# Top-k attention and a tanh-shrink layer on one core: weights turned by VectorE in 32x32 blocks, value products on eight tiles of TensorE

## The chip, the cores and the metric

The program runs on one core of one Trainium2 chip. The metric is device time in microseconds (us) for one execution, from the first to the last instruction with what the launch adds around it. A change under 0.2% of this kernel's time can't be told from no change.

A core has four engines that compute, TensorE (matrix products and transposes), VectorE, ScalarE and GpSimd, and a fifth, SyncE, that here only issues DMAs. Each works through its own instructions in order and waits on semaphores for the others. The profile calls them PE, DVE, ACT, POOL and SP; PEld is TensorE's loading of the stationary operand, which it lists apart from the products.

## The reference

Two blocks, one after the other, all in float32. The first is attention over 8 batches, 8 heads, 576 positions and head size 64, which keeps for each query the 32 largest scores; the second is a feed-forward layer of width 2048 on the 4608 rows of 512.

```python
scores = scale * np.matmul(q, k.transpose(0, 1, 3, 2))
kth = np.partition(scores, -top_k, axis=-1)[..., -top_k:-top_k + 1]
scores = np.where(scores >= kth, scores, -1000000000.0)
attn = np.exp(scores - np.max(scores, axis=-1, keepdims=True))
attn = attn / (np.sum(attn, axis=-1, keepdims=True) + 1e-09)
attn_out = np.matmul(attn, v)
x = attn_out.transpose(0, 2, 1, 3).reshape(4608, 512)
h = x @ w_in
out = (h - np.tanh(h)) @ w_out
```

## The kernel before

**Steps.** The unit of attention is a step: 128 queries of one pair of heads `hp` in one batch `b`. A batch has four pairs. 576 queries are four blocks of 128 (`qt` 0 to 3) and a rest of 64; a rest step (`rem`) takes the 64 last queries of two head pairs together. That makes 18 steps for a batch (16 and two rests) and 144 in all. `plan` (L462) puts them in order: for each batch the blocks 0 and 1 of the four pairs, then the two rest steps, then the blocks 2 and 3.

**A step's way through the engines.** `scores` (L198) forms 128 x 576 scores for both heads in four matmuls into the PSUM tile `scps`, and ScalarE copies them to `sc` (L215). `search` (L218) is VectorE's part: it splits the 576 keys into two halves, takes the larger and the smaller of each pair (L237, L238, which read `scps` and `sc`), and finds the threshold with four rounds of eight maxima (L245) and replacements (L248). `mask` (L255) sets what lies below the threshold far down (ScalarE L277, GpSimd L280), `expo` (L289) takes the exponential in place in `z` and its sum. `weigh` (L328) turns the 128 x 576 weights of each head so that keys lie on partitions: nine transposes on TensorE through PSUM (L346, L352), copied out by ScalarE to `et` and `e4` (L349, L353). `values` (L357) runs once for two blocks (256 queries) or for a rest step: for each head four matmuls with 128 keys and one with 64 (L374), the two heads side by side in the two column halves of the array, then one or two transposes that spread the reciprocal of the sums (L382), a copy (L386) and a product on GpSimd (L396).

**The feed-forward layer** works on units of 256 rows: 18 units, each 16 items `ffn_h` (four matmuls, L416) and 16 items `ffn_o` (two matmuls, L436). A unit becomes ready when the last pair of heads of its two blocks is through `values`. `deal` (L534) spreads its items over the steps that follow.

**Order.** The program's order is written out by hand in `run` (L485); there is no scheduler. In iteration `n` of its main loop each engine gets, in this order: the turning of step n-2 (first part), `mask` of n-1, `search` of n, four tenths of the step's feed-forward items, `scores` of n+1, the rest of the turning of n-2, `expo` of n-1, two tenths, `values` of n-2, two tenths, what is due in `todo` (loads, and the turning of keys and queries in `turn_kq`, L173), two tenths. `between(i)` is called in `search` after round i.

**The first 17 steps** also convert the feed-forward weights, which come as raw words: 32 pieces in all, one piece in each of the steps 0 to 8, four in step 9, three in each of the steps 10 to 16. A piece is two loads issued by ScalarE's queue (`raw` L117, `shifted` L119), and in a first part (part 1) VectorE L129 and L133 and ScalarE L130, L131, L136, in a second (part 2) VectorE L139 and GpSimd L142. Loads run three pieces ahead: when a piece's second part is through, the load of the third next is issued. Feed-forward items wait for the pieces that they need.

**Loads.** SyncE loads keys, queries and values for each pair of heads once (`load_kq` L156, eight DMAs; `load_v` L165, four DMAs). The values of a pair stay for all its steps, in four buffers.

Matmuls in float32 stand twice in the profile: L436 has 18 x 32 = 576 matmuls in the program and 1152 rows, each a load of the stationary operand and a product. Such a row is called a pass here. Transposes take one pass.

At the end VectorE checks that the search in halves found the true threshold everywhere; if not, everything is run again exactly. That second run does not take place with these inputs.

Of the kernel before, what the change touches and what calls it, by code (L numbers as in the profile page):

```python
# [19 lines left out]
J = 4  # L20
# [22 lines left out]
def kernel(  # L43
# [19 lines left out]
    CF = DFF // P  # L63
    WJ = 4
# [15 lines left out]
    mpool = pool("m", 3)  # L80
    zpool = pool("z", 2)
    etpool = pool("et", 1)
# [4 lines left out]
    rawpool = pool("raw", 3)  # L87
    shpool = pool("shifted", 3)
# [58 lines left out]

    raw, kT, qT, vb, vr = {}, {}, {}, {}, {}
# [4 lines left out]
    def main_rows(src, b, h):  # L153
        return src[b, h, 0:JP, :].rearrange("(p j) d -> p j d", j=J)

    def load_kq(b, hp):  # L156
        for name, src in (("k", k), ("q", q)):
            x = ldpool.tile([P, J + 1, 2, D], FP32, tag=f"{name}in", name=f"{name}in")
            for t in range(2):
                h = 2 * hp + t  # L160
                nc.sync.dma_start(x[:, 0:J, t, :], main_rows(src, b, h))
                nc.sync.dma_start(x[0:R, J, t, :], src[b, h, JP:S, :])
            raw[name, b, hp] = x

    def load_v(b, hp):  # L165
        x = vb[b, hp] = kqpool.tile([P, 2, J, D], FP32, tag="vb", name="vb")
        y = vr[b, hp] = kqpool.tile([P, D], FP32, tag="vr", name="vr")
        for t in range(2):
            h = 2 * hp + t
            nc.sync.dma_start(x[:, t, :, :], main_rows(v, b, h))  # L170
            nc.sync.dma_start(y[half(t), :], v[b, h, JP:S, :])

    def turn_kq(b, hp):  # L173
        p4 = None
        for name, dst in (("k", kT), ("q", qT)):
# [3 lines left out]
            for c in range(J):  # L179
# [3 lines left out]
            p4 = zt_ps.tile([P, 512], FP32, tag="zt", name="kqps")  # L183
            nc.tensor.transpose(  # L184
                p4[:, 0:R], x[0:R, J, :, :].rearrange("p h d -> p (h d)"), ident[0:R, 0:R]
            )

            for rows, o in [(half(0), 0), (half(1), R)] if name == "k" else [(slice(0, P), 0)]:
                nc.scalar.copy(d[rows, o : o + JP], ps[rows, :])
                o = 0 if o else JP  # L190
                nc.scalar.copy(d[rows, o : o + R], p4[rows, 0:R])
            yield

    st = {}

    def scores(n):  # L198
        g = steps[n]
        ps = sc_ps.tile([P, 2, 2, 512], FP32, tag="sc", name="scps")  # L200
        for s in range(2):
            ks = slice(s * S2, (s + 1) * S2)
            for i in range(2 if g.rem else 1):
                qs = slice(JP, S) if g.rem else slice(g.qt * P, (g.qt + 1) * P)
                rows = half(i) if g.rem else slice(0, P)
                for t in range(2):
                    nc.tensor.matmul(  # L207
                        ps[rows, t, s, 0:S2],
# [6 lines left out]
        nc.scalar.copy(sc[:], ps[:, :, :, 0:S2])  # L215
        st[n] = dict(sc=sc, ps=ps)

    def search(n, exact, between):  # L218
# [6 lines left out]
        sc, ps = x["sc"], x.pop("ps")  # L225
# [6 lines left out]
        else:  # L232
# [4 lines left out]
            nc.vector.tensor_tensor(lo, ps[:, :, 0, 0:S2], sc[:, :, 1, :], ALU.min)  # L237
            nc.vector.tensor_tensor(hi, ps[:, :, 0, 0:S2], sc[:, :, 1, :], ALU.max)  # L238
# [87 lines left out]
    ets = {}  # L326

    def weigh(n):  # L328


        g, z = steps[n], st[n]["z"]
        if g.rem:
            o = 0
        else:
            o = (g.qt % 2) * P
        if o:
            et, e4 = ets[n - 1]
        else:
            et = etpool.tile([P, 2, J, N], FP32, tag="et", name="et")
            e4 = etpool.tile([P, N], FP32, tag="e4", name="e4")  # L340
        ets[n] = et, e4
        for t in range(2):
            zt = zt_ps.tile([P, 512], FP32, tag="zt", name="zt")
            m0 = t * (S + R)
            for c in range(J):
                nc.tensor.transpose(  # L346
                    zt[:, c * P : (c + 1) * P], z[:, m0 + c * P : m0 + (c + 1) * P], ident[:]
                )
            nc.scalar.copy(et[:, t, :, o : o + P], zt[:].rearrange("p (c j) -> p c j", c=J))  # L349
# [135 lines left out]
    def run(exact):  # L485
# [32 lines left out]
        for piece in pieces[:3]:  # L518
            next(piece)
# [105 lines left out]
```

## Time and profile before

| | us |
|---|---|
| median of 3 runs (1764.85 to 1766.08) | 1765.44 |
| the profiled execution | 1765.89 |
| its span, first to last instruction | 1764.0 |

| engine | busy us | share of the span | instructions |
|---|---|---|---|
| PE | 1628.9 | 92% | 8418 |
| PEld | 1041.7 | 59% | 8418 |
| DVE | 1159.9 | 66% | 3635 |
| ACT | 1086.1 | 62% | 2133 |
| POOL | 893.2 | 51% | 1369 |

The groups that the change touches, of the list of the costliest groups (out<-in, count, busy us, mean ns of one):

| line, engine | what | count | busy us | mean ns |
|---|---|---|---|---|
| L346 PE | transposes of the weights | 1152 | 159.1 | 283 |
| L352 PE | the same, last 64 keys | 144 | 48.0 | 333 |
| L349 ACT | their copy out of PSUM | 288 | 156.8 | 597 |
| L353 ACT | the same, last 64 keys | 144 | 38.8 | 270 |
| L374 PE | value products, 128 keys | 1536 | 148.0 | 336 |
| L374 PE | value products, last 64 keys | 384 | 53.7 | 358 |
| L382 PE | spreading the reciprocals | 144 | 34.3 | 312 |
| L386 ACT | copy of products and reciprocals | 80 | 43.5 | 544 |

How to read it: an engine's busy time is the union of its instructions' spans, so where passes overlap, the mean of one is longer than what each adds. For TensorE the chain of waits is the better measure: it follows the end of the program back to what held each step up, and gives each pass the time by which it moved the chain on.

### The profile page before, as it was taken

Reading aid. Unit: us, or ns where it says so; the run is one execution under the profiler, and the core shown is the slowest. Engines: PE = TensorE matmul, PEld = TensorE weight load, DVE = VectorE, ACT = ScalarE, POOL = GpSimd, SP = SyncE. Lnnn points to the kernel's source line nnn. Section 1 sums busy time; section 2 is a strip of 40 time slices with the busy share of each in tenths; the row PEclk is TensorE's granted clock in tenths of the full one; section 3 lists DMA queues with packets and bytes.
Section 4 is the critical chain, followed back from the end, with each engine's and each line's share of the span. In section 5 each row is a group of like instructions: output and inputs, shape, how many; then the busy total and the mean of one; then the engine's idle time right before and its main releaser. Section 6 shows DMA issues by size and latency. Waiting matters only on the chain.

```text
span 1764.0 us, 25564 instructions
## 1 busy us (share of the span) xinstructions
PE 1628.9 (92%) x8418; PEld 1041.7 (59%) x8418; DVE 1159.9 (66%) x3635; ACT 1086.1 (62%) x2133; POOL 893.2 (51%) x1369
## 2 busy tenths in 40 slices
PE   3645669999999999999999999999999999999998
PEld 2324435657574757575666565757475756575664
DVE  5886777678767777733767786678766876752700
ACT  3766666657675767644666576757675767643631
POOL 1555654646454645542545464647454655542621
PEclk9777789999999999999999999999999999999999
DMA  5434422100210011000020002100110011000000
GB/s 179 129 108 174 171 102 58 30 13 1 50 44 13 1 46 48 8 7 13 21 53 21 13 8 53 34 13 1 47 47 7 7 34 47 6 7 13 1 12 14
DMA packets 106765, 73.03 MB, mean 41 GB/s; under 512 B 85632, under 2 KB 93824, under 8 KB 106624
## 3 DMA queue, kind: packets, MB, share of 16 engines
q1 hardware_dynamic: 97408, 37.78, 8.3%
q10 hardware_dynamic: 9216, 33.54, 5.3%
q8 instruction: 68, 1.11, 0.2%
q14 instruction: 73, 0.60, 0.1%
HBM read 61.85 MB, written 9.44 MB: 40 GB/s over the span
## 4 chain that ended last, share of the span: by engine, by line
PE 86%; DVE 7%; ACT 4%; issue 1%; ACTq 1%; POOL 0%; DMA 0%; SPq 0%; DVEq 0%; POOLq 0%
PE ops L436 28%; PE hps L416 27%; PE av L374 10%; PE scps L207 8%; PE zt L346 7%; DVE m L245 2%; PE zt L352 2%; PE av L382 2%; DVE ab L248 2%; DVE f L139 1%; PE kqps L180 1%; ACT sc L215 1%; ACT z L277 1%; PE kqps L184 1%; ACTq L119 0%
## 5 line engine op out<-in xcount | busy, mean ns | idle before, releaser
L280 POOL TENSOR_TENSOR z<-sc,z 128x576 f32<-128x576 f32 x288 | 401.8, 1417 | 283.0 <-ACT z L277 283.0
L436 PE MATMUL ops<-w_out,g 128*128 128x512 f32 x1152 | 530.3, 598 | 0.0
L416 PE MATMUL hps<-xT,w_in 128*128 128x256 f32 x2048 | 477.9, 384 | 0.0
L245 DVE MAX8 m<-ab 128x8 f32<-128x288 f32 (+1 forms) x1152 | 467.9, 448 | 0.0
L416 PEld LDWEIGHTS hps<-xT,w_in 128*128 128x128 f32 x2048 | 384.2, 194 | 47.6 <-issue 0.5
L248 DVE MATCH_REPLACE8 ab<-m,ab 128x288 f32<-128x288 f32 x864 | 375.8, 443 | 0.0
L436 PEld LDWEIGHTS ops<-w_out,g 128*128 128x128 f32 x1152 | 208.8, 194 | 192.0 <-issue 188.8
L430 POOL TENSOR_TENSOR g<-g,th 128x512 f32<-128x512 f32 x144 | 183.6, 1275 | 205.2 <-ACT g L429 200.5
L277 ACT ACTIVATE z<-sc,tbs 128x576 f32<-128x576 f32 x288 | 208.2, 775 | 51.7 <-POOL tbs L264 51.7
L293 ACT ACTIVATE z<-z,nb 128x576 f32<-128x576 f32 x288 | 222.7, 779 | 15.1 <-POOL z L280 15.1
L215 ACT COPY sc<-scps 128x1152 f32<-128x1152 f32 x144 | 160.3, 1113 | 116.3 <-ACT z L277 46.5
L349 ACT COPY et<-zt 128x512 f32<-128x512 f32 x288 | 156.8, 597 | 97.7 <-PE zt L346 97.3
L314 DVE RECIPROCAL rd<-rd 128x4 f32<-128x4 f32 x64 | 11.3, 177 | 310.2 <-POOL rd L307 310.1
L346 PE MATMUL zt<-ident,z 128*128 128x128 f32 x1152 | 159.1, 283 | 49.7 <-ACT z L293 29.8
L207 PE MATMUL scps<-kT,qT 64*128 64x288 f32 (+1 forms) x1280 | 188.1, 447 | 8.4 <-DVE ab L238 8.0
L237 DVE TENSOR_TENSOR ab<-scps,sc 128x576 f32<-128x576 f32 x144 | 106.6, 740 | 134.3 <-ACT sc L215 100.8
L346 PEld LDWEIGHTS zt<-ident,z 128*128 128x128 f32 x1152 | 139.9, 146 | 91.5 <-ACT z L293 31.6
L428 ACT ACTIVATE th<-hps 128x512 f32<-128x512 f32 x144 | 85.3, 593 | 144.5 <-PE hps L416 125.9
L207 PEld LDWEIGHTS scps<-kT,qT 64*128 64x128 f32 (+1 forms) x1280 | 101.0, 184 | 100.5 <-issue 33.9
L374 PE MATMUL av<-et,vb 128*64 128x256 f32 (+1 forms) x1536 | 148.0, 336 | 0.0
L374 PEld LDWEIGHTS av<-et,vb 128*64 128x64 f32 x1536 | 86.4, 139 | 62.3 <-ACT e L353 12.9
L240 DVE MAX8 ab<-ab 128x8 f32<-128x288 f32 x288 | 116.8, 447 | 0.0
(62 smaller groups left out, 1360.2 us busy)
## 6 DMA issues: line engine op xcount, KB each, us to landing
raw<-in_moe_w_in_dram ACTq DMA_DIRECT2D x16, 512.0 KB, 3.7
kin<-in_k_dram SPq DMA_DIRECT2D x64, 128.0 KB, 2.6
qin<-in_q_dram SPq DMA_DIRECT2D x64, 128.0 KB, 2.6
vb<-in_v_dram SPq DMA_DIRECT2D x64, 128.0 KB, 2.3
raw<-in_moe_w_out_dram ACTq DMA_DIRECT2D x16, 512.0 KB, 3.6
out_dram<-ot SPq DMA_DIRECT2D x32, 256.0 KB, 2.2
shifted<-in_moe_w_in_dram ACTq DMA_DIRECT2D x16, 511.5 KB, 4.6
shifted<-in_moe_w_out_dram ACTq DMA_DIRECT2D x16, 511.5 KB, 4.5
```

What stands on the lines that cost most here:

```text
L207: nc.tensor.matmul(ps[rows, t, s, 0:S2], qT[g.b, g.hp + i][half(t), qs], kT[g.b, g.hp + i][half(t), ks], start=True, stop=True,)
L215: nc.scalar.copy(sc[:], ps[:, :, :, 0:S2])
L245: nc.vector.max(m[:, t, m8], last[t] if i == rounds - 1 else cur[t])
L248: nc.vector.match_replace(nxt[t], m[:, t, m8], cur[t], NEG)
L277: nc.scalar.activation(zv[:, t, :], scf[:, t, :], AF.Relu, bias=tbs[:, t, n : n + 1], scale=-BIG)
L280: nc.gpsimd.tensor_tensor(zv[:, t, :], scf[:, t, :], zv[:, t, :], ALU.subtract)
L293: nc.scalar.activation(x["zv"][:, t, :], x["zv"][:, t, :], AF.Exp, bias=x["nb"][:, t : t + 1], scale=scale, accum_out=den[:, t : t + 1],)
L346: nc.tensor.transpose(zt[:, c * P : (c + 1) * P], z[:, m0 + c * P : m0 + (c + 1) * P], ident[:])
L374: nc.tensor.matmul(av[half(t), 0, cols], vb[g.b, hp][:, t, c, :] if c < J else vr[g.b, hp][rows, :], et[:, t, c, cols] if c < J else e4[ro ...
L416: nc.tensor.matmul(ps[:, f % 2, :], w_in[j][:, c, fo : fo + P], u.xT[:, c, :], start=(c == 0), stop=(c == CD - 1),)
L430: nc.gpsimd.tensor_tensor(g, g, th[:], ALU.subtract)
L436: nc.tensor.matmul(cur[u][:], u.g[f // FJ][:, f % FJ, i * P : (i + 1) * P], w_out[f // FJ][:, f % FJ, :], start=(f == 0), stop=(f == CF - 1),)
```

## The change

- **Turning the weights.** `weigh` is gone, with its nine transposes on TensorE and three copies on ScalarE for each step. `turn_z` puts one VectorE instruction in their place, which turns `z` (128 partitions x 1152 elements) into `zt` block by block: each block of 32 x 32 is turned within itself. It is issued inside `search` of step n, after the first round, for step n-2.
- **Value products.** In `zt` a row group of 32 partitions holds 32 keys of a block of keys and, along the free dimension, 32 queries for each of the 18 blocks of keys. `values` now makes for each block of keys (18), each group of 32 queries (4 row groups of the array) and each head (2 column halves) a matmul of 32 keys x 64 values with 64 queries (32 in a rest step): 144 matmuls where there were 10 (20 in a rest step). The four row groups write four PSUM banks.
- **PSUM.** `scps` and the products share one tile `acc` of four banks: scores in columns 0 to 287 of each bank, products in two places by turns behind them. The reciprocals are turned into a buffer of their own (`rb`), so that there are two copies instead of one.
- **Values held four times.** Each row group needs all keys on its own 32 partitions, so `load_v` loads `v` four times, with 12 DMAs for each use (two steps of a pair), 64 uses, into two buffers. It is called when the use before the last is through.
- **Keys and queries.** The last 64 rows of keys and queries are loaded into one tile `last` and turned together: three DMAs instead of four, one transpose instead of two, and six copies become four.
- **Order of the steps.** The rest steps come one by one, behind the second and the fourth pair of the blocks 2 and 3 (in the last batch of the blocks 0 and 1).
- **Loads of the feed-forward weights** run two pieces ahead instead of three, in two buffers each.

```diff
-    rawpool = pool("raw", 3)
-    shpool = pool("shifted", 3)
+    rawpool = pool("raw", 2)
+    shpool = pool("shifted", 2)
...
     def load_v(b, hp):
-        x = vb[b, hp] = kqpool.tile([P, 2, J, D], FP32, tag="vb", name="vb")
-        y = vr[b, hp] = kqpool.tile([P, D], FP32, tag="vr", name="vr")
-        for t in range(2):
-            h = 2 * hp + t
-            nc.sync.dma_start(x[:, t, :, :], main_rows(v, b, h))
-            nc.sync.dma_start(y[half(t), :], v[b, h, JP:S, :])
+        x = vb[b, hp] = vpool.tile([P, 2, KB, D], FP32, tag="vb", name="vb")
+        hs = slice(2 * hp, 2 * hp + 2)
+        for a in range(NG):
+            for t in range(2):
+                h = 2 * hp + t
+                nc.sync.dma_start(
+                    x[group(a), t, 0 : J * J, :].rearrange("i (g c) d -> i g (c d)", c=J),
+                    v[b, h, 0:JP, :].rearrange("(g i c) d -> i g (c d)", g=J, c=J),
+                )
+            nc.sync.dma_start(
+                x[group(a), :, J * J : KB, :].rearrange("i t c d -> i t (c d)"),
+                v[b, hs, JP:S, :].rearrange("h (i c) d -> i h (c d)", c=2),
+            )
...
+    acc = sc_ps.tile([P, 2, 2, 512], FP32, name="acc")
...
-        ps = sc_ps.tile([P, 2, 2, 512], FP32, tag="sc", name="scps")
...
-    ets = {}
-    def weigh(n):
...
+    zts = {}
+    def turn_z(n):
+        g, z = steps[n], st.pop(n)["z"]
+        i = 0 if g.rem else g.qt % 2
+        zts[n] = zts[n - 1] if i else ztpool.tile([P, 2, 2 * S], FP32, tag="zt", name="zt")
+        nc.vector.transpose(zts[n][:, i, :], z[:])
...
     def values(n):
...
-            for c in range(J + 1):
+        turns[0] ^= 1
+        o = S2 + turns[0] * 2 * G
+        cols = slice(o, o + nq * G)
+        for kb in range(KB):
+            slot = kb if kb >= J * J else kb % J * J + kb // J
+            for a in range(NG):
+                x = vb[g.b, g.hp + (a // 2 if g.rem else 0)]
                 for t in range(2):
-                    rows = slice(0, P) if c < J else half(t)
                     nc.tensor.matmul(
-                        av[half(t), 0, cols],
-                        vb[g.b, hp][:, t, c, :] if c < J else vr[g.b, hp][rows, :],
-                        et[:, t, c, cols] if c < J else e4[rows, cols],
-                        start=(c == 0),
-                        stop=(c == J),
+                        acc[half(t), a // 2, a % 2, cols],
+                        x[group(a), t, slot, :],
+                        zt[group(a), 0:nq, t * S + kb * G : t * S + (kb + 1) * G],
+                        start=(kb == 0),
+                        stop=(kb == KB - 1),
+                        tile_position=(a * G, t * D),
                     )
+        rb = zt_ps.tile([P, 512], FP32, tag="zt", name="rb")
...
-        nc.scalar.copy(xs[:, :, 0:w], av[:, :, 0:w])
+        w = nq * P
+        nc.scalar.copy(
+            xs[:, 0, 0:w].rearrange("p (i a j) -> p a i j", i=nq, a=NG),
+            acc[:, :, :, cols].rearrange("p u w (i j) -> p (u w) i j", i=nq),
+        )
+        nc.scalar.copy(xs[:, 1, 0:w], rb[:, 0:w])
...
-                if a == 0:
-                    steps.extend([Step(b, hp, J) for hp in range(0, NHP, 2)])
+                    if hp % 2 and a == (b < B - 1):
+                        steps.append(Step(b, hp - 1, J))
...
+            at(uses[i - 2][2] if i > 1 else i - 2, lambda b=b, hp=hp: load_v(b, hp))
...
-                    if k + 3 < len(pieces):
-                        next(pieces[k + 3])
-            if i == 0 and 0 <= n - 2 and n < EARLY:
-                invert(n - 2)
+                    if k + 2 < len(pieces):
+                        next(pieces[k + 2])
+            if i == 0 and n >= 2:
+                if n < EARLY:
+                    invert(n - 2)
+                turn_z(n - 2)
...
-                w = weigh(n - 2)
-                next(w)
```

## The prediction, made before the changed kernel was run

> **What bounds the kernel now.** I began with the engines' busy shares (PE 92%), which are a mean over unlike stages, and so took the busy time by stretch next: the steps that convert weights, the steady stage, the tail. Columns: stretch, its length, then busy us and instructions of PE, PEld, DVE, ACT and POOL, the granted clock, the DMA share, GB/s.
> ```profile
> 0.00:264.00 264.00, 142.61 (x706) 93.26 (x707) 190.67 (x512) 165.74 (x305) 134.87 (x178) 0.78 0.43 144
> 264.00:1700.00 1436.00, 1429.31 (x7516) 911.39 (x7515) 969.10 (x3122) 909.97 (x1810) 748.16 (x1183) 1.00 0.09 24
> 1700.00:1764.00 64.00, 56.99 (x199) 37.03 (x197) 0.14 (x1) 10.34 (x19) 10.15 (x8) 0.98 0.05 14
> ```
> For 1436 us TensorE has no gap; there a us taken from it is a us won, whatever the others do. In the first 264 us no engine is full and a chain through several sets the pace; the granted clock is 0.78. The tail is the last unit's feed-forward, which the change leaves alone.
>
> Third, the chain of waits, steady stage (shares of 1436 us) and first stage (of 264):
> ```profile
> by line: PE ops L436 32.1%; PE hps L416 31.0%; PE av L374 11.6%; PE scps L207 10.2%; PE zt L346 8.0%; PE zt L352 2.3%; PE av L382 1.7%; PE kqps L180 1.5%; PE kqps L184 0.7%; ACT xs L386 0.2%; ACT qT L189 0.2%; ACT kT L189 0.2%; issue 0.1%;
> ```
> ```profile
> by line: DVE m L245 12.8%; DVE ab L248 10.4%; DVE f L139 9.9%; ACT sc L215 6.7%; issue 5.5%; ACT z L277 4.2%; PE ops L436 3.2%; PE zt L346 2.9%; ACTq L119 2.8%; DVE w_out L133 2.7%; DVE f L129 2.6%; DMA kin<-in_k_dram 2.4%; PE av L374 2.3%;
> ```
> The first says what the turning (8.0 + 2.3%) and the products (11.6%) cost; the second that VectorE is the longest part of the early chain, so that what is put on it there adds time.
>
> **The change part by part: steady stage.** *Removed.* Turning: 10.3% of 1436 = 148 us. Old products: 11.6% = 167 us over 72 calls (8 of the 80 fall in the first stage), 2.3 us a call. One kqps transpose fewer for each pair: about half of L184's 0.7%, 5 us. Together 320 us.
>
> *Added on TensorE.* A call of `values` is now 144 matmuls, 288 passes, of 32 rows x 64 columns of the array with 64 moving columns. Let X be what a call costs. In work for the array it is small: eight such passes fill the array once. The trace shows passes on separate parts side by side. Of the rest step's scores four passes (64x64, in four quarters) start together:
> ```profile
> 965.86:965.88 0.03, 0.02 (x4) 0.03 (x4) 1.00 0.00 0
> ```
> that is, four products (first bracket) and four loads within 0.03 us. All sixteen take this (from the chain):
> ```profile
> 965.93 1.13 PE scps L207 x16
> ```
> 1.13 / 4 = 0.28 us for a group of four with 288 columns, 63 ns for 64 columns. Now 288 / 8 = 36 groups: 36 x 63 ns = 2.3 us, the low end. The nearest row in size is the rest step's products, 64 columns, two halves side by side (timeline):
> ```profile
> 1012.26 0.69 PE L374 MATMUL av<-et,vb 128*64 128x64 f32 x16
> 1012.87 0.33 PE L374 MATMUL av<-e,vr 64*64 64x64 f32 x4
> ```
> The second form starts 0.61 us after the first, so eight pairs take 76 ns each; 36 x 76 = 2.7 us if eight go as two do. If no more than two go side by side it is 288 x 38 ns = 11 us, the far end; if no more than four, 72 x 63 to 76 ns = 4.5 to 5.5.
>
> *Supply of instructions.* The program has to be brought in too.
> ```profile
> q8 instruction: 68, 1.11, 0.2%
> ```
> 1.11 MB on q8 over TensorE's 16,836 rows (products and loads) is 66 B a row, in packets of 16 KB; that q8 is TensorE's is my inference from these sizes. A call is now 576 rows, 38 KB, 2.3 packets. How long one takes to land no row shows; the nearest, a 16 KB load of `vr`, lands 2.1 us after its issue, so 2.1 x 2.3 = 4.8 us a call if each is waited for in full, nothing if they come ahead. No stretch of before asks for instructions at such a rate: sixteen passes in 0.61 us are only 2 KB. Between 2.7 (hidden) and 4.8 (not) neither row is nearer; I take about the middle, X = 3.6, and keep 2.3 to 5.5 for the range: 72 x 3.6 = 259 us.
>
> *A rule that speaks against it.* The row first: the sixteen passes above took 38 ns each, four others started within 30 ns. The Trainium skill, "TensorE: Matmul & The Clock Gate", section "Wait — 56ns, not 53.3ns?", says that start-to-start of matmuls never falls below about 25 ns, however small they are. By it, as an estimate, a call is 288 x 25 = 7.2 us, 72 calls 518 us, and the sum below 2054. The row's 38 ns is no proof that passes can come faster.
>
> *The product's new waits.* `values` of n-2 sits on TensorE's queue behind the scores of n+1. It now waits for `turn_z`, issued in the search of n, and, since scores and products share `acc`, for the copy `sc` of step n+1; in turn the next search's first operation (L257) waits for the copy of the products (L390). Between scores and `values` lie two tenths of the feed-forward items, which cover the copy. By the hand-written order 14 of the 72 calls have none there; the copy's wait of some 1.3 us is then open: 19 us, and with the new waits behind it I put down 25.
>
> *VectorE, ScalarE, GpSimd.* VectorE gets one turn of 128 x 1152 a step. No row has it: the 128x512 operation of L133 takes 0.488 on `w_in`, so 1.1 us; L139 takes 0.996 for 512, so 2.2. Between, by L133 and a little over, 1.25. VectorE is busy 969 us of 127 steps, 7.6 of 11.3 us; 3.7 are spare, which hide even 2.2. ScalarE loses L349 and L353 (157 + 39 us) and is not on the steady chain; the copy L390/L394 is two instructions for one, hidden behind the next feed-forward items. The `z` buffer of n-2 comes free after the turn, inside search n; its next writer, `mask` of n, stands an iteration later on ScalarE and GpSimd. GpSimd: no change. All three at nothing, covered by TensorE's passes.
>
> *Queues.* SyncE issues 12 DMAs for each use of v in place of 4 for each pair (32 pairs); 64 uses of four copies of 295 KB are 75 MB in place of 9.4, beside the page's 73 in all. At about 0.5 us an issue it is 6.5 us a use, every two steps (22 us), beside `load_kq` and the outputs, which stand behind them on SyncE's queue. Behind a rest step 24 issues stand together, 13 us, plus 2.3 to land, and they are due two steps (22 us) later: hidden with 7 us to spare. The DMA share is 0.09, and its doubling has room. The rest steps' new places and the keys' three DMAs move work and do not change it: nothing.
>
> Steady stage: -320 + 259 + 25 = -36 us.
>
> **The first stage.** Here the same edits lie on a chain. Waits there (engine and line, what released it; us, times, longest):
> ```profile
> DVE ab L237 <- ACT sc L215: 52.7, 16, 17.9
> DVE f L139 <- ACT f L131: 19.2, 9, 7.1
> ACT sc L215 <- DVE f L139: 21.9, 9, 3.9
> ```
> VectorE waits for the scores' copy at each step's start, and then works through search and conversion.
> - Turns: 17 x 1.25 = +21 us on the engine that carries the chain (16 to 38 by its ends).
> - Values between `sc` and L257: the search of n+1 now waits for the products of n-2, since these stand between. 8 calls x (3.6 + 0.45 for the copy) = +32 (nothing if feed-forward work or conversion is later; 50 at X = 5.5).
> - Loads two pieces ahead: `raw` lands after 3.7 us, `shifted` after 4.5. In the steps 10 to 16, with three pieces, the load for the third piece is issued only when the first's part 2 is through, right before its own part 1: about 4.5 us open in each of 7 steps and 4 in step 9, +35 (nothing if ScalarE's queue issues it earlier than I read).
> - ScalarE's copies, 17 x (2 x 0.6 + 0.3) = 25 us, of which the chain had about 11: -11.
> - What falls into waits that VectorE has anyway (52.7 us above): -12.
>
> Together +65, bounds 10 to 110. TensorE's turning here (2.9%) is among what the new `values` replaces.
>
> **Sum** on the profiled execution, 1765.9 (0.45 above the median 1765.4; nothing to correct): -36 + 65 = +29, about **1795 us**. In X: the total is 1536 + 72 X, equal to before at X = 3.2.
>
> **The rivals.**
> 1. *Instructions come ahead of need* (the other side): X is 2.4 to 2.9, and the total 1536 + 173 to 209, 1709 to 1745. For it: q8's share is 0.2%, and passes in separate parts start together. Against: 38 KB within 3 us is a rate that no stretch shows. It decides wherever X stays under 3.2.
> 2. *Supply waited for in full, or only four passes at a time*: X 4.8 to 5.3, 1882 to 1918. For it: no row shows more than four together. Against: TensorE runs on between calls for 8 us, in which packets could come.
> 3. *Only two at a time, or a floor for each pass*: X of 7 to 11, 2040 to 2330. Against: the four starts within 0.03 us.
> 4. *The first stage hides it*: the wait of 52.7 us takes in the calls, loads come in time; only turns less copies, +10. With X = 3.6: 1740.
> 5. *The change does not do what it says*: VectorE becomes the steady bound. It would need a turn over 3.7 us, above both rows; each us above costs 127, so 1922 at 4.7.
>
> **How the numbers follow.** Forecast (X 3.2 to 4.4, first stage near +65; 1765 to 1850): 0.42. Rival 1: 0.29. Rival 2: 0.15. Rival 4: 0.07. Rival 3: 0.05. Rival 5: 0.02. A change under 0.2% (3.5 us) can't be told from none. Faster: rivals 1 and 4, 0.36. Same: 0.05, the forecast's edge near X = 3.2. Slower: the remaining 0.59. The range runs from rival 1's low end with a larger steady gain, 1702, to within rival 2, 1900; beyond lie rival 3, most of 5 and the upper part of 2. The forecast's own range is 1765 to 1850.
>
> **What would show it.** In the profile after: the chain's share of L375 in the steady stage over 72 calls is X, under 3.2 or over; zt gone from TensorE; q8 near 56,420 rows x 66 B = 3.7 MB. If supply binds, gaps between passes of L375 come at distances of about 250 rows (16 KB); if tiles bind, they are even. L353 on VectorE near 1.25 us. In the first stage L257 waiting for L390 in place of L235, and `f` L133 and L137 waiting for the loads of `raw` and `shifted`. A first stage not near 329 us, or an X far from 3.6, makes me wrong; two errors of opposite sign could leave the total near 1795 all the same.

## The result, and the profile after

The changed kernel takes 2125.5 us (four runs, 2122.6 to 2131.8) against 1765.7: 1.204 times as long, with a 95% interval of 1.202 to 1.207. The forecast was 1795, its range 1702 to 1900. The profiled execution's span is 2123.7 us.

The busy time by stretch of the kernel after, with the ends moved to where its stages lie (columns as before: length, busy us and instructions of PE, PEld, DVE, ACT, POOL, granted clock, DMA share, GB/s):

```profile
0.00:368.00 368.00, 142.41 (x2680) 99.89 (x2681) 212.38 (x528) 150.50 (x260) 132.44 (x177) 0.64 0.41 127
368.00:2060.00 1692.00, 1485.79 (x25337) 1000.78 (x25336) 1133.62 (x3251) 748.91 (x1438) 747.13 (x1184) 0.91 0.21 55
2060.00:2123.70 63.70, 56.18 (x197) 36.74 (x195) 0.14 (x1) 10.34 (x19) 10.11 (x8) 0.98 0.05 15
```

The tail is as it was. The first stage is longer, the steady stage is longer, and two things are new there: TensorE is no longer always busy (1486 of 1692 us), and its granted clock is 0.91 where it was 1.00. The chain of waits over the steady stage:

```profile
by line: PE ops L444 29.0%; PE hps L424 22.6%; PE acc L375 15.7%; issue 12.6%; PE acc L227 6.9%; ACT sc L235 2.3%; PE rb L385 2.0%; PE kqps L200 1.7%; POOL g L438 1.6%; POOL z L300 1.2%; ACT z L297 1.1%; ACT g L437 0.8%; ACT th L436 0.7%; P
```

The turning is gone from it. The products (L375) have 15.7%, and "issue", 0.1% before, has 12.6%: time in which TensorE waited for nothing that the profile shows. The timeline of one call of `values` shows where most of that is (start, us, engine and line, in brackets the idle time ahead):

```profile
1322.69 1.87 PE L375 MATMUL acc<-zt,vb 32*64 32x64 f32 x153
1326.77 1.58 PE L375 MATMUL acc<-zt,vb 32*64 32x64 f32 x128 [2.21 <-issue]
1330.79 0.48 PE L375 MATMUL acc<-zt,vb 32*64 32x64 f32 x7 [2.44 <-issue]
1331.20 0.69 PE L385 MATMUL rb<-ident,rx 128*128 128x128 f32 x2
```

Of the call's 288 passes 153 go by in 1.9 us, then nothing for 2.2 us, then exactly 128, nothing for 2.4 us, and the last 7. 128 passes are 256 rows (a load and a product each), and that is one of q8's packets:

```profile
q8 instruction: 224, 3.67, 0.7%
```

3.67 MB over 224 packets is 16.4 KB each; over 56,420 rows it is 65 B a row, so 252 rows a packet. Every one of the 72 calls of the steady stage has such a hole (over 0.7 us from start to start), 19 of them two, 128 passes apart. The 128 passes that end with a hole take, hole included, 3.47 us in the median of all 80 calls.

That the packet ends the hole can be read from the trace's DMA records. From 1326 to 1331 us, with the second hole in it, a single packet moves on the core's DMA engines, and it is q8's:

```profile
DMA packets 1, 0.02 MB, mean 3 GB/s; under 512 B 0, under 2 KB 0, under 8 KB 0
q8 instruction: 1, 0.02, 1.1%
```

It is under way from 1328.4 to 1329.3 us, and the passes go on at 1330.8. All 88 holes between the search of the 19th step and that of the last one are like this: the passes go on 1.2 to 1.6 us after the end of a q8 packet, 2.4 us (median) after its start. In the hole shown no other DMA moves, so the fourfold loads of `v` are not what holds the packet up there.

The clock round the same call:

```profile
1326.00:1328.00 2.00, 1.24 (x115) 1.24 (x120) 0.00 (x0) 0.00 (x0) 0.00 (x0) 1.00 0.00 0
1328.00:1330.00 2.00, 0.35 (x31) 0.21 (x22) 0.00 (x0) 0.00 (x0) 0.00 (x0) 0.70 0.03 8
1330.00:1334.00 4.00, 3.21 (x12) 1.79 (x13) 2.27 (x5) 0.74 (x2) 1.62 (x5) 0.50 0.02 4
1334.00:1336.00 2.00, 2.00 (x8) 1.14 (x7) 2.00 (x7) 0.59 (x2) 0.12 (x1) 0.59 0.00 0
1336.00:1340.00 4.00, 4.00 (x21) 3.26 (x21) 4.00 (x14) 2.58 (x6) 2.43 (x2) 1.00 0.62 164
```

The clock falls to 0.50 during the second hole and stays there for some seven us, and the feed-forward products behind the call run at half speed meanwhile: products of L444 start 0.85 us apart at 0.50 and 0.43 us apart at 1.00 (medians). Of the 54 times that the clock falls to 0.50 between the 19th and the last search, 50 begin within 6 us of the start of a hole; in the kernel before it stays at 1.00 there.

An account of TensorE makes the steady stage add up. It takes the distances between the starts of successive products, from the search of the 19th step to that of the last one, puts each down to the line that it begins with, up to 0.7 us, and counts the rest of a longer one as a gap, by what comes behind it.

| us, 19th to last search | before | after | difference |
|---|---|---|---|
| value products | 160 | 302 | +142 |
| gaps inside a call of `values` | 0 | 116 | +116 |
| turning of the weights | 132 | 0 | -132 |
| feed-forward products | 896 | 969 | +74 |
| the same, what lies above 0.7 us | 0 | 15 | +15 |
| gaps ahead of the products | 0 | 24 | +24 |
| scores | 146 | 151 | +5 |
| everything else | 64 | 67 | +2 |
| together | 1398 | 1644 | +246 |

70 calls lie between these two searches, so a call costs (302 + 116) / 70 = 6.0 us of TensorE. The feed-forward products are the same work; the 74 us are the clock, and nearly all of the 15 too, since a product of L444 at 0.50 takes the 0.85 us of above, more than the 0.7 that are counted for one.

In the first stage VectorE's own waits say it (kernel after, 0 to 368 us; us, times, longest):

```profile
DVE ab L257 <- ACT xs L390: 80.5, 8, 12.8
DVE ab L257 <- ACT sc L235: 35.8, 10, 17.8
DVE f L133 <- DMA raw<-in_moe_w_out_dram: 19.3, 5, 4.5
DVE f L133 <- DMA raw<-in_moe_w_in_dram: 8.4, 3, 4.2
DVE w_out L137 <- DMA shifted<-in_moe_w_out_dram: 4.9, 6, 0.9
DVE f L143 <- ACT f L135: 3.8, 2, 2.4
DVE w_in L137 <- DMA shifted<-in_moe_w_in_dram: 2.9, 3, 1.2
```

From the start to the search of the 18th step it takes 368.0 us where it took 265.7. VectorE's idle time ahead of the search's first operation is 116.3 instead of 52.7 (+63.6), that of the loads 35.5 instead of nothing, the 15 turns take 20.3, and the old waits fell by 18.4 (L139's 19.2 to 3.8, the reciprocals' 3.0 to 0): +101 of the 102.

### The profile page after: what moved, and what is told of

Same layout as the page of the kernel before. It is cut to its first block, busy times and chain, and to the rows that moved or that the text cites. A ratio compares the mean times of both kernels' runs of the same rounds, so it can differ in the third digit from the quotient of the medians.

```text
span 2123.7 us, 65651 instructions
## 1 busy us (share of the span) xinstructions
PE 1684.4 (79%) x28210; PEld 1137.4 (54%) x28210; DVE 1346.1 (63%) x3779; ACT 909.8 (43%) x1717; POOL 889.7 (42%) x1369
## 3 DMA queue, kind: packets, MB, share of 16 engines
q8 instruction: 224, 3.67, 0.7%
## 4 chain that ended last, share of the span: by engine, by line
PE 67%; issue 11%; DVE 9%; ACT 6%; POOL 3%; DMA 3%; ACTq 1%; DVEq 0%; POOLq 0%
PE ops L444 25%; PE hps L424 20%; PE acc L375 14%; PE acc L227 6%; ACT sc L235 3%; DVE m L265 2%; DVE ab L268 2%; PE rb L385 2%; DMA shifted<-in_moe_w_out_dram 1%; POOL g L438 1%; PE kqps L200 1%; DVE f L143 1%; ACT z L297 1%; POOL z L300 1%; DVE zt L353 1%
## 5 line engine op out<-in xcount | busy, mean ns | idle before, releaser
L444 PE MATMUL ops<-w_out,g 128*128 128x512 f32 x1152 | 574.7, 648 | 16.7 <-POOL w_out L146 15.1
L375 PE MATMUL acc<-zt,vb 32*64 32x64 f32 (+1 forms) x23040 | 311.3, 248 | 311.6 <-issue 180.3
L424 PE MATMUL hps<-xT,w_in 128*128 128x256 f32 x2048 | 506.0, 405 | 11.4 <-ACT g L437 10.8
L375 PEld LDWEIGHTS acc<-zt,vb 32*64 32x64 f32 x23040 | 284.7, 145 | 373.5 <-issue 199.0
L257 DVE TENSOR_TENSOR ab<-acc,sc 128x576 f32<-128x576 f32 x144 | 107.3, 745 | 513.3 <-ACT xs L390 477.6
L444 PEld LDWEIGHTS ops<-w_out,g 128*128 128x128 f32 x1152 | 230.2, 209 | 283.1 <-issue 261.9
L235 ACT COPY sc<-acc 128x1152 f32<-128x1152 f32 x144 | 160.9, 1117 | 238.3 <-issue 172.8
L227 PE MATMUL acc<-kT,qT 64*128 64x288 f32 (+1 forms) x1280 | 191.7, 451 | 65.7 <-DVE ab L258 43.4
L313 ACT ACTIVATE z<-z,nb 128x576 f32<-128x576 f32 x288 | 221.4, 773 | 11.0 <-POOL z L300 11.0
L353 DVE STREAM_TRANSPOSE zt<-z 128x1152 f32<-128x1152 f32 x144 | 196.8, 1366 | 4.1 <-PE acc L375 4.1
L404 POOL TENSOR_TENSOR xT<-xs 128x256 f32<-128x256 f32 x64 | 46.6, 728 | 352.2 <-ACT xs L394 352.2
L227 PEld LDWEIGHTS acc<-kT,qT 64*128 64x128 f32 (+1 forms) x1280 | 103.6, 186 | 157.4 <-issue 56.8
```

The source lines that it names most:

```text
L227: nc.tensor.matmul(acc[rows, t, s, 0:S2], qT[g.b, g.hp + i][half(t), qs], kT[g.b, g.hp + i][half(t), ks], start=True, stop=True,)
L235: nc.scalar.copy(sc[:], acc[:, :, :, 0:S2])
L313: nc.scalar.activation(x["zv"][:, t, :], x["zv"][:, t, :], AF.Exp, bias=x["nb"][:, t : t + 1], scale=scale, accum_out=den[:, t : t + 1],)
L353: nc.vector.transpose(zts[n][:, i, :], z[:])
L375: nc.tensor.matmul(acc[half(t), a // 2, a % 2, cols], x[group(a), t, slot, :], zt[group(a), 0:nq, t * S + kb * G : t * S + (kb + 1) * G], ...
L424: nc.tensor.matmul(ps[:, f % 2, :], w_in[j][:, c, fo : fo + P], u.xT[:, c, :], start=(c == 0), stop=(c == CD - 1),)
```

## The experiments

A time without an interval is that of one execution; those of the changed kernel span 9 us, so smaller differences are not read from these.

**Half of the products.** Is it the instructions? The first run halves them; it leaves out the second half of the keys.

```diff
-        for kb in range(KB):
+        for kb in range(KB // 2):
...
-                        stop=(kb == KB - 1),
+                        stop=(kb == KB // 2 - 1),
```

> Only the first 9 of the 18 blocks of keys are multiplied in values (72 matmuls a call, 144 passes; the second half of the products is left out). Theory S (instructions come in packets of 16 KB, 128 passes of a product and a load each; one packet is fetched ahead, and the next one's fetch takes some 3.4 us from the moment the packet before is used up, so a first boundary in a call is free and a later one costs about 2 us): 144 passes meet one boundary, free, so a call costs the array's part alone, 1.5 to 1.8 us instead of 5.8, long gaps between passes of L375 nearly go, the granted clock in the steady stage is back near 1.00 instead of 0.91, and the time is about 2125 - 72 x 4.2 - 80 (the clock's part) - 30 (first stage) = 1710. Rival T (each 128 passes cost about 2 us whenever they come, or the array itself is slow): a call costs half of 5.8, 2.9, with a long gap in most calls, and the time is about 1870 to 1900.

Measured: 1729.0 us. Windows of the steady stage (340 to 1680 us) and the page's clock row:

```profile
340.00:1680.00 1340.00, 1278.14 (x15017) 836.61 (x15016) 1122.29 (x3233) 746.99 (x1438) 748.09 (x1181) 0.98 0.26 69
PEclk9955666899999999999999999999999999999999
```

The holes nearly go (10 us instead of 116; 61 of the 72 calls have none), a call falls from 6.0 to 2.0 us, and the clock is back. The feed-forward products fall from 969 to 921 us without being touched. Halving the passes took away two thirds of a call's cost, as theory S has it: a first packet lies ready, the next does not.

**The same instructions, a quarter of the work.** Here the array gets less to do, TensorE's queue as many instructions as before.

```diff
+            w8 = G if kb == 0 else G // 4
...
-                        acc[half(t), a // 2, a % 2, cols],
+                        acc[half(t), a // 2, a % 2, cols].rearrange("p (i j) -> p i j", i=nq)[:, :, 0:w8],
...
-                        zt[group(a), 0:nq, t * S + kb * G : t * S + (kb + 1) * G],
+                        zt[group(a), 0:nq, t * S + kb * G : t * S + kb * G + w8],
```

> The changed kernel with the same number of matmuls, but from the second block of keys on each takes 16 moving columns instead of 64 (three quarters of the products are left out), so that the array has about a quarter of the work and the instructions are as many. Theory S (the supply of instructions sets what a call costs): long gaps between passes of L375 stay, one or two a call and longer rather than shorter since the rows before them are used up sooner; a call goes from 5.8 to no less than 4.8 us, the clock stays near 0.9, and the time lies between 2050 and 2130. Rival T (the array's columns): a call costs 2.5 to 3 us, and the time is 1830 to 1900.

Measured: 2173.3 us, longer than with all columns. The page's group and the windows from 380 to 2100 us:

```profile
L376 PE MATMUL acc<-zt,vb 32*64 32x16 f32 (+2 forms) x23040 | 294.8, 228 | 322.1 <-issue 193.9
```
```profile
380.00:2100.00 1720.00, 1504.88 (x25187) 1013.67 (x25187) 1124.63 (x3224) 743.34 (x1425) 740.87 (x1174) 0.87 0.21 54
```

A call costs 289 + 126 = 415 us / 70 = 5.9 us, nearly the 6.0 that it cost with 64 columns; the median from hole to hole is again 3.47 us. So the columns hardly matter and the instructions do: 256 rows per 3.47 us is what TensorE gets. The time lies above the expected range because of the clock, which fell further, from 0.91 to 0.87 (feed-forward products 1004 us, 35 more). There are as many holes (88), and each is a little longer (2.2 instead of 2.0 us in the median), since less work stands between them; which of the two lowers the clock the run doesn't show.

**Three parts with feed-forward work between.** If a packet comes while something else runs, the holes can be covered.

```diff
+            if kb and kb % 6 == 0:
+                yield
...
-                values(n - 2)
+                for _ in values(n - 2):
+                    force(2)
```

(`force` issues up to two feed-forward items and takes them from what later portions get.)

> All products, in three parts of 48 matmuls, with up to two feed-forward items (some 1.8 us each, few instructions) between the parts. Theory S: while an item runs the next packet comes, so the long gaps between passes of L375 go, a call costs 3.0 to 3.3 us of TensorE, the clock in the steady stage is near 1.00; 72 x 2.6 = 190 and about 80 of the clock less, the first stage as it is since there are few items there: about 1850. Rival T (a cost of the passes themselves): gaps and clock stay, 2100 to 2130.

Measured: 2267.2 us, slower still. The holes did go: 8 us are left of 116, and the products cost 257 us, 3.7 a call. But two waits took their place (waits from 385 to 2169 us):

```profile
DVE ab L257 <- ACT xs L392: 647.9, 71, 38.6
...
PE acc L227 <- DVE ab L258: 210.5, 106, 6.5
```

The search cannot begin before the products of an earlier step are copied, since scores and products share `acc`; the call is now longer from end to end, and TensorE itself waits for that search with its next scores. Gaps ahead of the scores are 175 us, where there were none.

**The search reads the copy alone.** This breaks that loop.

```diff
-            nc.vector.tensor_tensor(lo, acc[:, :, 0, 0:S2], sc[:, :, 1, :], ALU.min)
-            nc.vector.tensor_tensor(hi, acc[:, :, 0, 0:S2], sc[:, :, 1, :], ALU.max)
+            nc.vector.tensor_tensor(lo, sc[:, :, 0, :], sc[:, :, 1, :], ALU.min)
+            nc.vector.tensor_tensor(hi, sc[:, :, 0, :], sc[:, :, 1, :], ALU.max)
```

On the changed kernel by itself:

> L257 and L258 read both halves of the scores from sc and none from acc, so that the search no longer waits for the products' copy. Theory C (in the first stage the products stand in the chain from one search to the next, which cost VectorE some 60 us more idle time at L257 than before): the wait of L257 for L390, 80 us in the first 377, goes, and the time falls by 45 to 65 us, nearly all in the first 17 steps: about 2070; the steady stage changes little, since TensorE is its bound. Rival D (TensorE's queue holds the chain together anyway: the next scores stand behind the products): 2110 to 2125.

Measured: 2125.3 us, no change. The first stage did get shorter, as theory C had it, though by less: L257 waits for no products any more, and the 19th search begins at 359.0 instead of 377.2. The steady stage gave it back: 1665 us instead of 1644, with 33 us of gaps ahead of the products instead of 24 and 10 us more in the feed-forward lines. Why these rose was not settled. In the first stage too part of the gain goes into other waits: VectorE waits 15.6 us for `zt`, where it did not, and 17.8 instead of 3.8 at L143. The time is rival D's, the mechanism half of C.

With the three parts:

> The products in three parts with up to two feed-forward items between, and the search reading sc alone. In the run with three parts alone the gaps between passes of L375 went (116 to 8 us) and a call fell to 3.6 us, but TensorE then waited some 215 us in the steady stage with the next scores (L227) for VectorE's L258, which waits for the products' copy. Theory S+C (stalls of the supply, and beside them the loop products, copy, search, next scores through the shared tile): with both taken away the steady stage falls by those 215 us and some 60 of the clock to about 1500, the first stage to about 340, and the time to about 1930. Rival (the wait only moves, since the scores still wait for the products' copy of acc): 2100 or more.

Measured: 2132.8 us. The gaps ahead of the scores went (175 to 11), 167 us ahead of the products came (46 before). VectorE now waits at another place (0 to 347 us, first two lines):

```profile
DVE ab L257 <- ACT sc L235: 50.8, 17, 16.8
DVE zt L353 <- PE acc L377: 33.7, 7, 8.4
```

over the steady stage 344 us in 62 waits: `zt` is there once, and the turn of the next pair waits for the last product. The wait had moved, as the rival said, though not for its reason: the scores hardly wait any more.

**That turn later, and the conversion in another order.** Two steps, one after the other. First the order in which the pieces' parts are issued, so that a load goes out one search round before it is needed:

```diff
-            seq = [(1, i) for i in mine[:1]]
-            for i in mine[1:]:
-                seq += [(1, i), (2, i - 1)]
-            seq += [(2, i) for i in mine[-1:]]
-            for x, (part, i) in enumerate(seq):
-                parts.setdefault((m, 3 * x // max(len(seq) - 1, 1)), []).append((part, i))
+            for x, i in enumerate(mine):
+                parts.setdefault((m, min(x, 3)), []).append((1, i))
+                parts.setdefault((m, min(x + 1, 3) if len(mine) > 1 else 3), []).append((2, i))
```

> As the run before it, and in the steps with several pieces a piece's second part comes before the next piece's first part, so that the load of the piece after next is issued one search round before it is needed. Theory (35 us of the first stage are waits for raw and shifted, since loads run two ahead): the waits of L133 and L137 for DMAs fall below 12 us and the time by 20 to 30. Rival (the wait turns up elsewhere in the chain, at the conversion's second part waiting for ScalarE, L143): within 8 us of the run before.

Measured: 2116.8, 16 us less, under the 20 to 30 expected; the 19th search begins 22 us earlier (341.4 instead of 363.8). The waits for loads fell from 40.5 us to 4.2:

```profile
DVE w_out L137 <- DMA shifted<-in_moe_w_out_dram: 2.4, 3, 0.8
...
DVE f L133 <- DMA raw<-in_moe_w_in_dram: 1.3, 3, 0.8
DVE f L133 <- DMA raw<-in_moe_w_out_dram: 0.5, 2, 0.3
```

Then the place of the turn:

```diff
-            if i == 0 and n >= 2:
-                if n < EARLY:
-                    invert(n - 2)
-                turn_z(n - 2)
+            if i == 0 and 2 <= n < EARLY:
+                invert(n - 2)
+            if n >= 2:
+                g = steps[n - 2]
+                if i == (1 if g.rem else 0 if g.qt % 2 else 3):
+                    turn_z(n - 2)
```

> As the run with three parts, sc alone and the other order of conversion (2117), with one thing moved: the turn that opens a new zt (first block of a pair, and the rest steps) comes later in the search (after its last round, for a rest step after its second), the turn that the products wait for stays after the first. Theory Z (with the stalls and the shared tile gone, the next loop is the single zt: VectorE's turn of the next pair waits for the last product, 344 us in all, and holds the search up): most of TensorE's idle 265 us in the steady stage goes, and the time is about 1870 to 1950. Rival (TensorE is idle for something else, or the wait moves to mask and its z buffers on ScalarE and GpSimd): 2060 or more.

Measured: 2107.6. VectorE's wait fell from 351 to 140 us, and the 166 us of gaps ahead of the products stayed: `zt` was not what held TensorE up. The rival's time; where it said the wait would move to `mask`, the trace shows the products waiting for ScalarE, 88 us for the copy `sc` and 92 us behind `expo` (L313). Feed-forward items stand in heaps, thirteen in a row in one place of the chain; that this is why the products wait is what the next run tries.

**Three parts between the usual portions.** So the forced items go, and the portions that are there anyway stand between.

```diff
-            deal(0.4)
+            parts3 = values(n - 2) if here(-2) else iter(())
+            whole = not here(-2) or not last_of_pair(n - 2)
+            deal(0.4 if whole else 0.2)
...
-            if here(-2):
-                values(n - 2)
+            next(parts3, None)
             deal(0.2)
+            if not whole:
+                next(parts3, None)
+                deal(0.2)
+                next(parts3, None)
```

> As the run with three parts, sc alone, the other order of conversion and the later turn (2108), but the parts stand between the usual portions of feed-forward items instead of forcing two items between them: the iteration's first portion is cut from four tenths to two, and the third part stands before the last portion. Theory F (in the forced runs TensorE's idle 264 us in the steady stage came of feed-forward items used up behind the products and then missing or standing in a heap, 13 in a row, elsewhere): the idle falls under 120 us, stalls stay under 40, and the time is 1900 to 2000. Rival (three parts make the products' chain too long whatever stands between): 2080 or more.

Measured: 1956.4 us, in the expected range and 151 less than the forced version. Windows from 332 to 1890 us:

```profile
332.00:1890.00 1558.00, 1438.07 (x25303) 951.55 (x25301) 1143.41 (x3225) 749.71 (x1425) 790.12 (x1175) 0.96 0.22 60
```

Holes are 25 us, gaps ahead of the products 66, the products 264, feed-forward work 960. It is the best of the versions that turn on VectorE with all products, and still 191 us slower than the kernel before: the products alone are 103 us above the old ones, while the turning that they replace was 132, and the gaps, the clock and a first stage longer by 59 us come on top.

**Two turns instead of one.**

```diff
-        nc.vector.transpose(zts[n][:, i, :], z[:])
+        for _ in range(2):
+            nc.vector.transpose(zts[n][:, i, :], z[:])
```

> turn_z is done twice in each step. Theory (VectorE's turn is hidden in the steady stage and lies on the chain in the first 17 steps): 16 x 1.37 = +22 us, about 2147, with the steady stage unchanged within 10 us. Rival (VectorE is close to the bound everywhere, since the products wait for it): 144 x 1.37 = +197 us, 2320.

Measured: 2207.3, 82 more, between the two. The first stage grew by 17 us, under the 22 expected; the steady stage by 63, where 10 were allowed. The gaps ahead of the products doubled (24 to 49 us), holes and products grew by 24, the feed-forward products by 11. VectorE is not full there (1300 of 1741 us), but by the program's order the search waits for the products' copy, the turn comes behind the search's first round, and the next products wait for the turn: a loop through VectorE that the kernel before did not have. That this loop makes the 63 us is argued, not shown: of the 49 us of gaps 3 end with the turn itself, 23 with ScalarE's copy `sc` and 20 with its L313.

**Two parts of the change on the kernel before.** The last keys and queries in one tile (two DMAs, one transpose for keys and queries; the keys in the order of before):

```diff
-                nc.sync.dma_start(x[0:R, J, t, :], src[b, h, JP:S, :])
+        for i, src in enumerate((k, q)):
+            nc.sync.dma_start(last[half(i)], src[b, hs, JP:S, :].rearrange("h r d -> r h d"))
...
-            nc.tensor.transpose(
-                p4[:, 0:R], x[0:R, J, :, :].rearrange("p h d -> p (h d)"), ident[0:R, 0:R]
-            )
+        nc.tensor.transpose(p4[:, 0:P], last[:].rearrange("p h d -> p (h d)"), ident[:])
```

> The kernel before with one part of the change alone: the last 64 keys and queries of a pair in one tile and one transpose (in the keys' order of before). Theory (in the steady stage what leaves TensorE is won): 28 pairs lose one L184 transpose and a PSUM tile, about 0.35% of the chain, 4 to 9 us less: 1757 to 1762. Rival: no difference that can be measured, since the larger transpose takes back what the smaller two cost.

Measured: 1746.8 us, 0.989 times the kernel before (0.988 to 0.991). TensorE's account falls from 1398 to 1379, 16 of it in the lines of these transposes and the reciprocals'. The groups, the kernel before in the first fence and this one in the second:

```profile
L184 PE MATMUL kqps<-ident,kin 64*128 64x64 f32 x32 | 9.1, 284 | 2.0 <-ACT xs L386 2.0
L184 PE MATMUL kqps<-ident,qin 64*128 64x64 f32 x32 | 9.0, 281 | 7.0 <-ACT e L353 7.0
```
```profile
L192 PE MATMUL kqps<-ident,last 128*128 128x128 f32 x32 | 9.4, 294 | 8.3 <-ACT e L357 8.3
```

32 passes instead of 64, each as long: 9 us. The other 7 of the account lie in the other transposes of keys and queries, 216 in both kernels, which with their waits take 23.5 us of it instead of 30.5. The 19 us are twice what was expected.

The rest steps in their new places alone:

```diff
+                    if hp % 2 and a == (b < B - 1):
+                        steps.append(Step(b, hp - 1, J))
...
-                if a == 0:
-                    steps.extend([Step(b, hp, J) for hp in range(0, NHP, 2)])
```

> The kernel before with the rest steps in their new places alone. Theory (same work, moved): within 5 us of the kernel before. Rival (the new order starves feed-forward work or piles it up at the end): over 20 us slower.

Measured: 1784.7 us, 1.010 times (1.008 to 1.012): neither nothing nor 20. In the steady stage TensorE now waits for the copies of the turned keys and queries (264 to 1700 us, this kernel):

```profile
PE zt L346 <- ACT kT L189: 12.2, 10, 1.7
PE zt L346 <- ACT qT L189: 6.9, 10, 1.0
```

19 us where it was 4.7. Another 6 us stand ahead of the 19th search (279.6 instead of 273.2).

The first of these with the search reading the copy alone:

> The kernel before with the last keys and queries in one tile (the run that took 1747), and with the search reading sc alone, so that PSUM's scores are free once ScalarE has copied them. Theory (TensorE, full in the steady stage, waits 8 us for L238 in the whole run, mostly in the first stage): 1735 to 1745. Rival (VectorE's two operations take as long, and the chain of the first stage runs through the copy in any case): 1745 to 1749.

Measured: 1748.1 us (0.990, 0.988 to 0.992), the rival: nothing is gained over 1746.8. The single tile for the last keys and queries is thus, of the parts tried alone, the one that makes the kernel before faster, by 1.1%.

## Why the prediction was wrong

It was right that TensorE is the steady stage's bound, that X, the cost of a call, decides, and that the point of balance is low. It was wrong in X, in one term that it did not have, and in the first stage. Of its two signs, gaps at distances of about 250 rows came (256 rows); the other, the chain's share of L375, would read 15.7% of 1692 us over 72 calls, 3.7 us, close to the forecast, because the chain books the holes as "issue". From 1795 to the profiled execution's 2125.6:

- **X, the supply of instructions.** The step "Between 2.7 (hidden) and 4.8 (not) neither row is nearer; I take about the middle, X = 3.6" failed. It treated the array's time and the packets' as rivals, of which the longer counts. They add: 288 passes need some 3.3 us without holes, 91 holes in 72 calls cost 2 us each, 2.5 a call, and 0.2 us lie behind the last pass; 6.0 in all. The landing of 2.1 us taken from a 16 KB load was too short as well: from a packet's start to the next pass it is 2.4 us, and packets come every 3.47. Rival 2 named the mechanism and priced it as 4.8 to 5.3, for the same reason too low. For the 70 calls of the account it is 418 us instead of 252: +166 us.
- **The clock.** The first fence of the prediction shows 1.00 in the steady stage and 0.78 in the first one, where TensorE has gaps. A change that makes gaps in TensorE's work could have been priced by that pair of numbers, and no step did. The feed-forward work, untouched, became 74 + 15 us longer. The run with half of the passes shows both at once: hardly any holes, clock back, 49 of the 74 us gone and 11 of the 15.
- **The first stage**, +65 forecast, +102 measured. Turns (+21 forecast, +20.3) and loads (+35, +35.5) were right in size. For the turns that is in part luck (17 of 1.25 us forecast, 15 of 1.35 measured); for the loads the mechanism was right too: the reordered conversion took those waits away. The chain through the products failed: +32 less 12 was put down, it was +63.6, since a call here costs 5.4 to 9.6 us from its first pass to its last at a clock of 0.64, and all of it stands between two searches. Old waits that fell are 18, where 11 were put down for ScalarE's copies. This is +37.
- **What was taken away.** The chain's shares gave 148 us for the turning and 167 for the products, 306 for the stretch with 70 calls; by the account above it is 132 and 160. That is +14. The products' new waits, put at 25, came as 24, in 29 calls instead of 14. The kq transposes were put at -5; alone they give -19, the rest steps' new places, put at nothing, +19.

166 + 74 + 15 + 37 + 14 = 306 of the 331 us; scores and spreading (+13) and the end behind the last search (+10) are most of the remainder.

"All three at nothing, covered by TensorE's passes" was right for the engines' busy time, and wrong for VectorE's place in the chain: a second turn costs 63 us in the steady stage. What was feared and did not come: passes on eight tiles do go side by side (the 3.3 us of a call without its holes are 11 ns a pass), so the far end of 11 us was far off, and the rule of "TensorE: Matmul & The Clock Gate" in the Trainium skill, section "Wait — 56ns, not 53.3ns?", that starts are never less than about 25 ns apart, does not hold for passes on separate tiles; their median distance here is 9 ns. SyncE's 12 DMAs a use cost the products no wait: none waits for `vb` in the trace.

The Trainium skill has a page that should have been set against the row, "Runtime: NRT & Kernel Launch", section "Instruction fetch mechanics": instructions come in 16 KiB blocks of 256, the next fetched while the current one runs, and crossing a block is "mostly hidden". The block's size agrees with the 128 passes between holes. That it is hidden holds here for one block in a row; passes of 11 ns use a block up in 1.4 us, and then 2 us stay open until the next one is in. It also gives TensorE's instruction memory as 128 KiB, eight such blocks; the runs show one lying ready.

## What to carry to other kernels

Count instructions as a resource with a rate of its own: here TensorE got 256 rows, 128 passes of a load and a product, every 3.47 us, 27 ns a pass, with 64 moving columns as with 16. By these runs, work cut into many small matmuls wants bursts of about a packet (144 passes: 10 us of holes in all) or long instructions between (parts of 96: 8 and 25 us); and a stall of TensorE costs twice, by itself and by the lower clock of what follows. When a product and a score are put into one PSUM tile to save banks, look for the loops that the shared tile closes before counting what the engines save: with the products in three parts this loop cost 134 us, with the products in one nothing.

## What the runs showed of the hardware

- One packet of 16 KB lies ready for TensorE: a call of 144 passes has no hole in 61 of 72 cases, one of 288 always has one or two. A hole ends 1.2 to 1.6 us after the end of a q8 packet, in 88 of 88 cases.
- With two holes of 2.2 and 2.4 us and 1.6 us of work between them the granted clock went to 0.50 for some seven us. With a quarter of the columns in the passes it fell to 0.87 over the stage, with as many holes.
- The turn of 128 x 1152 elements in blocks of 32 x 32 takes VectorE 1.37 us, 1.2 ns an element of the free dimension:

```profile
L353 DVE STREAM_TRANSPOSE zt<-z 128x1152 f32<-128x1152 f32 x144 | 196.8, 1366 | 4.1 <-PE acc L375 4.1
```
